# A transformer block on one core: memory pieces in a bank of their own, one filling rate, and another order at the start

## The chip, the cores and the metric

The kernel runs on one core of a Trainium2 chip. The metric is the device time of one execution in microseconds (us), less is better. The engines are named as the profile names them: PE (TensorE, matmuls), PEld (its weight loads), DVE (VectorE), ACT (ScalarE), POOL (GpSimd) and SP (SyncE, which here only issues DMAs). Each engine works through its own queue in order; semaphores tie the queues together. SBUF is the on-chip memory, PSUM the eight banks into which PE writes its results.

## The reference

One block with adaptive layer norm, an attention with a compressive memory, and a gated linear unit. x has 2048 rows of 512; there are 32 heads of 16; the rows form 4 segments of 512. All is fp32.

```python
mod = (silu(c) @ w_mod).reshape(1, 6, 1, 512)      # sa, ca, ga, sb, cb, gb
h = layernorm(x) * (1 + ca) + sa
q, k, v = heads(h @ wq), heads(h @ wk), heads(h @ wv)
for s in range(4):                                  # segments, in order
    logits = qs @ ks.T * 16 ** -0.5 + causal_mask
    a_dot  = softmax(logits) @ vs
    a_mem  = (phi(qs) @ M) / (phi(qs) @ z + 1e-6)   # phi(t) = t + 1 if t > 0 else exp(t)
    out[s] = g * a_mem + (1 - g) * a_dot            # g = sigmoid(beta)
    M, z   = M + phi(ks).T @ vs, z + sum(phi(ks))
x = x + ga * (out @ wo)
h = layernorm(x) * (1 + cb) + sb
x = x + gb * (((h @ w_gate) * (h @ w_up)) @ w_down) # 1376 inner columns
```

## The kernel before

**Accuracy.** Matmuls of the projections and of the GLU part run in a reduced fp32 format, each operand split into a high and a low half (names ending in H and L), so each product is three matmuls: high x high, low x high, high x low. Query and key go to DRAM as three bf16 parts each and come back stacked along the contraction.

**Stages.** At the start (L400 to L702) the kernel loads x of segment 0, the first two modulations (wm0), and the projection weights, in the order v, k, q. `mod0` (L464) makes shift and scale, `ln` (L107) the normalized and transposed h of segment 0, `load_w` (L481) the halves of the weights (ACT rounds the high half, POOL, for two pieces of v DVE, subtracts). Then PE computes V of segment 0 (`a_v`, L498) and key and query of head group 0 (`a_kq`, L518). A head group is 8 heads, 128 columns; there are 4 in a segment, and `a_kq(s, g, nm)` also makes phi of key or query for the memory.

Then comes the attention loop (L708). A *unit* is 4 heads of one segment; there are 32 units, and the loop variable v is the unit whose keys are worked on. Each turn has five *slots*. In a slot stand, in PE's order: query logits for the maxima of a later unit (`q_step`, L190: matmuls q<-kst,qst and, at the end of the slot, the mask matmuls q<-cmask), key logits of unit v (`k_step`, L244; ACT takes the exponential L262, POOL cuts the triangle L265), the products with V (`av_step`, L269, tile tb), and then the filling. `q_step` writes one PSUM tile of two banks (tag lq, one buffer), and DVE's reduction L226 (tile mxb) empties it; the next slot's q waits for that. In slot 2 `n_step` (L230) transposes the maxima into the bank sm (tile ntp), in slot 4 `t_step` (L293) transposes the output there (tile tr).

**The filling.** What else PE must do is written as generators that yield an estimated cost in us: `fill_a` (L630) for the segments' norms, projections and memory, `fill_b` (L649) for the weights of wo, the output projection (`wo_seg`, tiles op and wops) and the second norm. After each slot `fill` (L672) adds rate/5 to a credit and takes pieces until it is used up. The rate is 10.0 before unit 0, 6.6 up to turn 22, and 4.8 from there. `until` forces what a coming unit needs. The order of all these matmuls on PE is fixed by a chain of dependencies (`pe`, L46); a scheduler orders the other engines' instructions.

**Memory pieces.** `a_mem(s, g)` (L560) has up to four: mp transposes phi(k) and ACT copies it (pkr); up 0 and up 1 multiply phi(q) with the memory MZ, and DVE's four operations L580 to L583 empty each into mem; mz multiplies pkr with V, and DVE (and POOL) add it to MZ. In `fill_a` all of `a_mem(s, g - 1)` follows the key projection of group g, that of the last group follows the next segment's norm. Each piece asks `bank` (L71) for a PSUM bank, as the projections do; in the loop that is the tag ms, two buffers in turn. V of the next segment comes before its first key projection, and waits (`vfree`) until the loop has left the buffers of V.

**The rest.** After the loop come the output projection of segment 3 and the GLU part (L754 to L796) over 4 segments and 11 column chunks.

Of the kernel before, what the change touches and what calls it, by code (L numbers as in the profile page):

```python
# [8 lines left out]
F32 = mybir.dt.float32  # L9
# [8 lines left out]
P = 128  # L18
S, D, H, DH, NSEG, L, F = 2048, 512, 32, 16, 4, 512, 1376
KT = D // P  # L20
NG = 4
HG = 8
# [9 lines left out]
def tile_kernel(ctx, tc, x, wq, wk_, wv, wo, beta, w_gate, w_up, w_down, c, w_mod, out):  # L32
# [74 lines left out]
    def ln(pool, hpool, xt, s, sc, sh, pfx, hb, fast):  # L107

        mv = pool.tile([P, 4, 2], F32, tag="mv", name=f"{pfx}mv{s}", bufs=2)
        for t in range(4):  # L110
            st = pool.tile([P, 6], F32, tag="st", name=f"{pfx}st{s}_{t}", bufs=2)
            nc.vector.bn_stats(st, xt[t])
            nc.vector.bn_aggr(mv[:, t, :], st)  # L113
        sd = pool.tile([P, 4], F32, tag="sd", name=f"{pfx}sd{s}", bufs=2)
        nc.scalar.activation(sd, mv[:, :, 1], AF.Sqrt, bias=epst[:, 0:1])
        y = pool.tile([P, 4], F32, tag="y", name=f"{pfx}y{s}", bufs=2)
        nc.vector.reciprocal(y, sd)
        a = pool.tile([P, 4], F32, tag="ya", name=f"{pfx}ya{s}", bufs=2)
        b = pool.tile([P, 4], F32, tag="yb", name=f"{pfx}yb{s}", bufs=2)
        eng = nc.gpsimd  # L120
        eng.tensor_mul(a, y, y)
        eng.tensor_scalar(b, mv[:, :, 1], 1.0, EPS, op0=ALU.mult, op1=ALU.add)  # L122
        eng.tensor_mul(b, b, a)
        eng.tensor_scalar(b, b, -0.5, 1.5, op0=ALU.mult, op1=ALU.add)
        eng.tensor_mul(y, y, b)
        yield 0.4
        for t in range(4):
            nc.vector.tensor_scalar(xt[t], xt[t], mv[:, t, 0:1], y[:, t:t + 1],
                                    op0=ALU.subtract, op1=ALU.mult)
        yield 0.4  # L130
        hH, hL = [], []
        for d in range(KT):
            ps = bank(f"{pfx}tp{s}_{d}")
            for t in range(4):
                TP(ps[:, t * P:(t + 1) * P], xt[t][:, d * P:(d + 1) * P], ident)
            h = pool.tile([P, L], F32, tag="hf", name=f"{pfx}hf{s}_{d}", bufs=hb[2])
            nc.scalar.activation(h, ps, AF.Identity, scale=sc[:, d:d + 1], bias=sh[:, d:d + 1])
            hi = hpool.tile([P, L], F32R, tag=hb[0].format(d), name=f"{pfx}hH{s}_{d}", bufs=hb[1])
            lo = hpool.tile([P, L], F32R, tag=hb[0].format(4 + d), name=f"{pfx}hL{s}_{d}", bufs=hb[1])
            if fast:  # L140
                nc.vector.tensor_copy(hi, h)
                nc.vector.tensor_sub(lo, h, hi.bitcast(F32))
            else:
                nc.scalar.activation(hi, h, AF.Copy)
                nc.gpsimd.tensor_sub(lo, h, hi.bitcast(F32))
            hH.append(hi)
            hL.append(lo)
            yield 0.45
        return hH, hL
# [40 lines left out]
    def q_step(u, i):  # L190
# [5 lines left out]
        def mm(c, h, qb, k0, n, b=None, stop=False):  # L196
            b = h % 2 if b is None else b
            MM(qp[:, b, c:c + n * P], Q[0:96, h, qb * P:(qb + 1) * P], K[0:96, h, k0 * P:(k0 + n) * P],
               start=True, stop=stop, skip_group_check=True)

        src = qp.rearrange("p b (j t) -> p (b j) t", t=P)
        if i == 4:
# [260 lines left out]

    def mod0():  # L464
        for j in range(2):
            a0 = mod_acc(r0[j])
            ps = bank(f"m0_{j}", shape=(P, 4))
            for i in range(4):
                MM(ps[:, i:i + 1], a0[:, i * P:(i + 1) * P], ones[:, 0:1], start=True, stop=True)
            nc.vector.tensor_copy(sa_c[:, 2 * j:2 * j + 2], ps[:, 0:2])  # L470
            nc.vector.tensor_scalar_add(ca_c[:, 2 * j:2 * j + 2], ps[:, 2:4], 1.0)

# [8 lines left out]
    def load_w(nm, w, nst):  # L481
        wH[nm] = [pa.tile([P, D], F32R, name=f"w{nm}H{k}", bufs=1) for k in range(KT)]
        wL[nm] = [pa.tile([P, D], F32R, name=f"w{nm}L{k}", bufs=1) for k in range(KT)]
        wr = w.rearrange("(k p) n -> p k n", p=P)
        for k in range(KT):
            tg, n = stage[(nst + k) % len(stage)]
            raw = pa.tile([P, D], F32, tag=tg, name=f"wr{nm}{k}", bufs=n)
            nc.sync.dma_start(raw, wr[:, k, :])
            hi, lo = wH[nm][k], wL[nm][k]
            if nm != "v":  # L490
                hi, lo, raw = (hi.rearrange("p (g d h) -> p g h d", g=NG, h=HG),
                               lo.rearrange("p (g d h) -> p g h d", g=NG, h=HG),
                               raw.rearrange("p (g h d) -> p g h d", g=NG, h=HG))
            nc.scalar.activation(hi, raw, AF.Copy)
            eng = nc.vector if nm == "v" and k % 2 == 1 else nc.gpsimd
            eng.tensor_sub(lo, raw, hi.bitcast(F32))

    def a_v(s):  # L498
        hH, hL = hcur[0]
# [18 lines left out]
    def a_kq(s, g, nm):  # L518
# [4 lines left out]
        if True:  # L523
# [14 lines left out]
            nc.scalar.activation(q3[:, 0, :], f, AF.Copy)  # L538
            (nc.vector if fast else nc.gpsimd).tensor_sub(r, f, q3[:, 0, :])
            (nc.vector.tensor_copy if fast else nc.scalar.copy)(q3[:, 1, :], r)  # L540
            nc.gpsimd.tensor_sub(q3[:, 2, :], r, q3[:, 1, :])
            for r0, n, k in ((0, 3, 0), (3, 2, 0), (5, 1, 0)) if nm == "k" else ((0, 1, 3), (3, 1, 2), (5, 1, 1)):
                if nm == "k":
                    nc.sync.dma_start(dst[s][g][r0:r0 + n].rearrange("r p t -> p r t"), q3[:, 0:n, :])
# [15 lines left out]
    def a_mem(s, g):  # L560

        ph = phs.pop((s, g))
        if s < NSEG - 1:
            mp = bank(f"mp{s}_{g}")
            for t in range(4):
                TP(mp[:, t * P:(t + 1) * P], ph["k"][:, t * P:(t + 1) * P], ident)
            pkr = pa.tile([P, 4, P], F32, tag="pkr", name=f"pkr{s}_{g}", bufs=1)
# [2 lines left out]
        if s > 0:  # L570
# [1 line left out]
            mem = pa.tile([P, 4, HG, DH], F32, tag="mem", name=f"mem{s}_{g}", bufs=1)  # L572
            gb = gg[:, g * HG:(g + 1) * HG]
            for i in range(2):
                up = bank(f"up{s}_{g}_{i}", shape=(P, 2, HG, VS))
                for t in (2 * i, 2 * i + 1):
                    MM(up[:, t % 2].rearrange("p h e -> p (h e)"), ph["q"][:, t * P:(t + 1) * P],
                       MZ[g].rearrange("p h e -> p (h e)"), start=True, stop=True)
# [6 lines left out]
                yield 0.5  # L585
            nc.sync.dma_start(memd[s][g], mem.rearrange("p t h e -> p (t h e)"))
        if s < NSEG - 1:
            mz = bank(f"mz{s}_{g}", shape=(P, HG, VS))
            for t in range(4):
                MM(mz.rearrange("p h e -> p (h e)"), pkr[:, t, :],  # L590
                   vt[s % 2][t][:, g * HG * VS:(g + 1) * HG * VS], start=t == 0, stop=t == 3)
# [24 lines left out]
    def open_b():  # L616
# [5 lines left out]
        for k in range(KT):  # L622
# [4 lines left out]
            nc.gpsimd.tensor_sub(woL[:, k, :], raw, woH[:, k, :].bitcast(F32))  # L627
            yield 0.3

    def fill_a():  # L630
        for s in range(NSEG):
            if s > 0:
                yield from a_ln(s)
                yield from a_mem(s - 1, NG - 1)
                while vfree[0] < s:
                    yield None
                yield from a_v(s)
                if s < 3:
                    yield from a_mod(s - 1)
            for g in range(1 if s == 0 else 0, NG):  # L640
                yield from a_kq(s, g, "k")
                if g > 0:
                    yield from a_mem(s, g - 1)
                if g == 2 and s + 1 < NSEG:
                    xts[s + 1] = xload(s + 1)
                yield from a_kq(s, g, "q")
        yield from a_mem(NSEG - 1, NG - 1)

    def fill_b():  # L649
        yield from open_b()  # L650
# [42 lines left out]
    next(lng)  # L693
    next(lng)
    mod0g()
    hcur[0] = run(lng)
    load_w("v", wv, 0)
    load_w("k", wk_, 4)
    load_w("q", wq, 8)
    run(a_v(0))  # L700
    run(a_kq(0, 0, "k"))
    run(a_kq(0, 0, "q"))  # L702
    btag[:] = ["ms"]
    load(0)
    load(1)
    until(0, 1)
    SL = 5.0
    for v in range(-2, NQ + 1):  # L708
        rate[0] = 10.0 if v < 0 else 6.6 if v < 23 else 4.8
        if 2 <= v + 3 < NQ:  # L710
            until((v + 3) // 8, (v + 3) // 2 % 4)
            load(v + 3)
# [112 lines left out]
```

## Time and profile before

| | us |
|---|---|
| three runs | 1060.09, 1062.77, 1066.46 |
| median | 1062.77 |
| profiled execution, whole | 1065.12 |
| its span, first to last instruction | 1063.4 |
| first query logits begin | 65.73 after the span's start |
| stretch from 692 to 1064, the GLU part | 372 |

The profile comes from one execution. The page gives the busy time of each engine and the share of the clock that PE was granted, in 40 slices; the list of waits gives, for two instructions, how long one engine sat idle until the other released it, how often, and the longest; a window's row gives for a stretch of the span the busy time and the number of instructions of each engine in turn, and at its end the granted clock, the share of the DMA engines and the GB/s. In a timeline a row is: start, length, engine, line, operation, out<-in, and in brackets the idle time before it with what ended it. The span is 1.7 us shorter than the execution's own time.

### The profile page before, as it was taken

How to read it: one execution, taken by the hardware profiler on the slowest of the kernel's cores; microseconds unless marked ns; L12 is line 12 of the kernel's file. 1: busy time of each engine (PE TensorE's matmuls, PEld its weight loads, DVE VectorE, ACT ScalarE, POOL GpSimd, SP SyncE). 2: the span in 40 equal slices, each digit the busy share in tenths (PEclk: the TensorE clock that was granted, in tenths of full speed). 3: DMA queues.
4: the chain of work that ended last, by engine and by line, in shares of the span. 5: the costliest groups of instructions: out<-in, count | busy, mean ns of one | idle time of the engine just before them, and what ended most of it. 6: DMA issues, size and time to landing. Idle time of an engine off the chain costs nothing.

```text
span 1063.4 us, 14282 instructions
## 1 busy us (share of the span) xinstructions
PE 946.1 (89%) x5496; PEld 656.4 (62%) x5496; DVE 495.8 (47%) x842; ACT 401.4 (38%) x564; POOL 301.2 (28%) x440
## 2 busy tenths in 40 slices
PE   5877998877988879998787989899999999999997
PEld 3555555554555544655444555688878878878885
DVE  8435564556554553555557554266523322322112
ACT  4335365553565553555435364223211211121111
POOL 6335143342153341354633242145400000000000
PEclk7789898989999987999799999999999999999999
DMA  7185334443244332255755422263220101011011
GB/s 235 48 254 165 93 116 124 144 154 102 79 154 144 100 105 66 77 167 182 238 174 154 122 71 74 73 180 90 83 80 1 40 15 65 3 38 40 1 40 39
DMA packets 83140, 109.81 MB, mean 103 GB/s; under 512 B 9504, under 2 KB 54560, under 8 KB 83072
## 3 DMA queue, kind: packets, MB, share of 16 engines
q1 hardware_dynamic: 82928, 108.89, 32.9%
q8 instruction: 43, 0.70, 0.3%
q14 instruction: 25, 0.20, 0.1%
q10 hardware_dynamic: 144, 0.02, 0.0%
HBM read 67.98 MB, written 40.63 MB: 102 GB/s over the span
## 4 chain that ended last, share of the span: by engine, by line
PE 73%; DVE 13%; DMA 5%; ACT 4%; issue 2%; POOL 2%; SPq 0%; DVEq 0%; ACTq 0%; POOLq 0%
PE gps L769 11%; PE ups L769 11%; PE q L54 10%; DVE mxb L226 7%; PE tb L54 6%; PE k L54 6%; PE vps L54 4%; PE qps L54 3%; PE kps L54 3%; PE wops L54 3%; PE acc3lq L782 1%; PE acc1lk L782 1%; PE acc1lq L782 1%; PE acc0lq L782 1%; PE acc2lk L782 1%
## 5 line engine op out<-in xcount | busy, mean ns | idle before, releaser
L226 DVE TENSOR_REDUCE mxb<-q 128x8 f32<-128x1024 f32 x160 | 195.6, 1223 | 215.3 <-PE q L54 215.2
L262 ACT ACTIVATE pt<-k 128x1024 f32<-128x1024 f32 x160 | 163.7, 1023 | 253.6 <-PE k L54 229.9
L265 POOL TENSOR_SCALAR_AFFINE_SELECT pt<-pt 128x256 f32<-128x256 f32 (+1 forms) x224 | 101.2, 466 | 282.2 <-ACT pt L262 280.2
L54 PE MATMUL q<-kst,qst 96*128 96x128 bf16 (+2 forms) x640 | 103.9, 287 | 52.4 <-DVE mxb L226 47.0
L774 DVE TENSOR_TENSOR gs<-gs,ups 128x512 f32<-128x512 f32 (+1 forms) x44 | 30.2, 687 | 187.9 <-PE ups L769 187.1
L54 PEld LDWEIGHTS <-qst 96*128 96x128 bf16 x640 | 52.6, 101 | 94.8 <-issue 86.4
L54 PE MATMUL k<-qst,kst 98*128 98x384 bf16 (+3 forms) x512 | 102.9, 315 | 2.2 <-ACT pt L262 2.1
L54 PE MATMUL tb<-pt,v 128*32 128x512 f32 (+3 forms) x1024 | 92.4, 457 | 0.5 <-POOL pt L265 0.5
L777 ACT ACTIVATE mH<-gs 128x512 fp32r<-128x512 f32 (+1 forms) x44 | 27.8, 631 | 160.8 <-DVE gs L774 160.8
L769 PE MATMUL ups<-chH,uH 128*128 128x512 f32 (+1 forms) x176 | 69.3, 394 | 0.0
L769 PE MATMUL gps<-chH,gH 128*128 128x512 f32 (+1 forms) x176 | 69.3, 395 | 0.0
L769 PE MATMUL ups<-chL,uH 128*128 128x512 f32 (+1 forms) x176 | 69.1, 393 | 0.0
L769 PE MATMUL gps<-chH,gL 128*128 128x512 f32 (+1 forms) x176 | 69.1, 392 | 0.0
L769 PE MATMUL gps<-chL,gH 128*128 128x512 f32 (+1 forms) x176 | 69.0, 392 | 0.0
L769 PE MATMUL ups<-chH,uL 128*128 128x512 f32 (+1 forms) x176 | 69.0, 392 | 0.0
L773 ACT ACTIVATE gs<-gps 128x512 f32<-128x512 f32 (+1 forms) x44 | 26.2, 599 | 107.0 <-PE gps L769 106.9
L54 PEld LDWEIGHTS <-kst 98*128 98x128 bf16 x512 | 48.0, 102 | 29.8 <-issue 9.6
L54 PEld LDWEIGHTS <-identb 128*128 128x128 bf16 x320 | 23.8, 101 | 64.9 <-issue 61.1
L54 PE MATMUL q<-cmask,identb 128*128 128x128 bf16 (+1 forms) x320 | 57.5, 263 | 0.0
L54 PEld LDWEIGHTS tb<-pt,v 128*32 128x32 f32 x1024 | 22.8, 111 | 37.3 <-issue 33.1
L778 DVE TENSOR_TENSOR mL<-gs,mH 128x512 fp32r<-128x512 f32 (+1 forms) x44 | 31.8, 723 | 28.2 <-ACT mH L777 28.1
L122 POOL TENSOR_SCALAR cyb<-cmv 128x4 f32<-128x4 f32 x4 | 0.8, 195 | 137.7 <-DVE cmv L113 137.6
(243 smaller groups left out, 1850.0 us busy)
## 6 DMA issues: line engine op xcount, KB each, us to landing
kst<-kd SPq DMA_DIRECT2D x32, 384.0 KB, 4.7
qst<-qd SPq DMA_DIRECT2D x32, 384.0 KB, 5.2
wm<-in_w_mod_dram SPq DMA_DIRECT2D x24, 256.0 KB, 3.2
kd<-k SPq DMA_DIRECT2D x16, 384.0 KB, 2.7
qd<-q SPq DMA_DIRECT2D x16, 384.0 KB, 2.7
x<-in_x_dram SPq DMA_DIRECT2D x16, 256.0 KB, 4.4
kd<-k SPq DMA_DIRECT2D x16, 256.0 KB, 2.1
qd<-q SPq DMA_DIRECT2D x16, 256.0 KB, 3.0
```

Source lines behind the costliest of these rows:

```text
L54: return pe(nc.tensor.matmul(*a, **k))
L122: eng.tensor_scalar(b, mv[:, :, 1], 1.0, EPS, op0=ALU.mult, op1=ALU.add)
L226: nc.vector.tensor_reduce(o, src, axis=AX.X, op=ALU.max)
L262: nc.scalar.activation(pt, kp, AF.Exp, scale=0.25)
L265: sels[u, i] = nc.gpsimd.affine_select(w, w, pattern=[[0, w.shape[1]], [1, P]], compare_op=ALU.is_ge, fill=0.0, base=0, channel_multiplier=-1)
L769: nc.tensor.matmul(ps[0:n], a[:, k, 0:n], b[k], start=j == 0, stop=j == 11)
L773: nc.scalar.activation(gs[0:n], pss[0][0:n], AF.Copy)
L774: nc.vector.tensor_mul(gs[0:n], gs[0:n], pss[1][0:n])
L777: nc.scalar.activation(mH[0:n], gs[0:n], AF.Copy)
L778: nc.vector.tensor_sub(mL[0:n], gs[0:n], mH[0:n].bitcast(F32))
L782: nc.tensor.matmul(acc[t], a[0:n, t * P:(t + 1) * P], b[0:n, :], start=i == 0 and j == 0, stop=i == NF - 1 and j == 2)
```

## The change

In words:

- `a_mem`: its tiles mp, up and mz are put into the tag sm (one buffer, that of ntp and tr) and no longer ask `bank`.
- `fill_a`: a new generator `inter(a, b)` takes a step of a, then a step of b, in turn. The memory pieces of the group before are taken in turn with the steps of a key projection, those of a segment's last group with the steps of the next segment's norm. V of segments 1 to 3 and the modulations move behind key and query of group 0.
- The filling rate is 5.7 in all turns from unit 0 on.
- Start: the weights are loaded in the order k, q, v; the k weights are asked for before the norm's transposes; key and query of group 0 come before V; group 1 is no longer forced ahead of the loop. All low halves of the weights are subtracted on DVE, and the last bf16 part of group 0's key and query too; five small operations of the first norm move from POOL to DVE.
- `mod0`: the weighted sum over the four blocks of wm0 is no longer made by DVE (eight operations) and followed by matmuls with a column of ones; each block is multiplied with its column of s_c on PE, four matmuls that accumulate.
- `q_step`: only the first matmul of a bank carries the start flag.

```diff
-        eng = nc.gpsimd
+        eng = nc.vector if pfx == "a" and s == 0 else nc.gpsimd
...
-               start=True, stop=stop, skip_group_check=True)
+               start=c == 0, stop=stop, skip_group_check=True)
...
     def mod0():
         for j in range(2):
-            a0 = mod_acc(r0[j])
             ps = bank(f"m0_{j}", shape=(P, 4))
             for i in range(4):
-                MM(ps[:, i:i + 1], a0[:, i * P:(i + 1) * P], ones[:, 0:1], start=True, stop=True)
+                for k in range(KT):
+                    MM(ps[:, i:i + 1], r0[j][k][:, i * P:(i + 1) * P], s_c[:, k:k + 1],
+                       start=k == 0, stop=k == KT - 1)
...
-            eng = nc.vector if nm == "v" and k % 2 == 1 else nc.gpsimd
-            eng.tensor_sub(lo, raw, hi.bitcast(F32))
+            nc.vector.tensor_sub(lo, raw, hi.bitcast(F32))
...
-            nc.gpsimd.tensor_sub(q3[:, 2, :], r, q3[:, 1, :])
+            (nc.vector if fast else nc.gpsimd).tensor_sub(q3[:, 2, :], r, q3[:, 1, :])
...
-            mp = bank(f"mp{s}_{g}")
+            mp = pst((P, 512), "sm", f"mp{s}_{g}")
...
-                up = bank(f"up{s}_{g}_{i}", shape=(P, 2, HG, VS))
+                up = pst((P, 2, HG, VS), "sm", f"up{s}_{g}_{i}")
...
-            mz = bank(f"mz{s}_{g}", shape=(P, HG, VS))
+            mz = pst((P, HG, VS), "sm", f"mz{s}_{g}")
...
+    def inter(a, b):
+        for w in a:
+            yield w
+            w = next(b, None)
+            if w is not None:
+                yield w
+        yield from b
+
     def fill_a():
+        mem = iter(())
         for s in range(NSEG):
             if s > 0:
-                yield from a_ln(s)
-                yield from a_mem(s - 1, NG - 1)
-                while vfree[0] < s:
-                    yield None
-                yield from a_v(s)
-                if s < 3:
-                    yield from a_mod(s - 1)
+                yield from inter(a_ln(s), mem)
+                mem = iter(())
             for g in range(1 if s == 0 else 0, NG):
-                yield from a_kq(s, g, "k")
-                if g > 0:
-                    yield from a_mem(s, g - 1)
+                if s == 0 and g == 1:
+                    mem = a_mem(0, 0)
+                yield from inter(a_kq(s, g, "k"), mem)
                 if g == 2 and s + 1 < NSEG:
                     xts[s + 1] = xload(s + 1)
                 yield from a_kq(s, g, "q")
-        yield from a_mem(NSEG - 1, NG - 1)
+                if s > 0 and g == 0:
+                    while vfree[0] < s:
+                        yield None
+                    yield from a_v(s)
+                    if s < 3:
+                        yield from a_mod(s - 1)
+                mem = a_mem(s, g)
+        yield from mem
...
     mod0g()
+    load_w("k", wk_, 0)
     hcur[0] = run(lng)
-    load_w("v", wv, 0)
-    load_w("k", wk_, 4)
-    load_w("q", wq, 8)
-    run(a_v(0))
+    load_w("q", wq, 4)
     run(a_kq(0, 0, "k"))
     run(a_kq(0, 0, "q"))
+    load_w("v", wv, 8)
+    run(a_v(0))
...
-    until(0, 1)
...
-        rate[0] = 10.0 if v < 0 else 6.6 if v < 23 else 4.8
+        rate[0] = 10.0 if v < 0 else 5.7
```

## The prediction, as it was put on record

> **What bounds the kernel now.** I read the page first, then what TensorE (PE) waits for, then the execution cut into stretches.
>
> ```profile
> PE 946.1 (89%) x5496; PEld 656.4 (62%) x5496; DVE 495.8 (47%) x842; ACT 401.4 (38%) x564; POOL 301.2 (28%) x440
> PEclk7789898989999987999799999999999999999999
> ```
>
> No engine is near full but PE, and PE's granted clock is below full only in the first two thirds. So there are two programs in one: a GLU part that PE fills, and an attention part with holes. The waits of PE say what the holes are:
>
> ```profile
> PE q L54 <- DVE mxb L226: 47.0, 58, 2.8
> PE mz L54 <- DVE mem L583: 18.5, 7, 3.0
> ...
> PE q L54 <- DMA qst<-qd: 4.6, 1, 4.6
> ...
> PE up L54 <- DVE phq L554: 3.1, 1, 3.1
> ```
>
> The first line is the cycle of the attention loop: one slot computes query logits (q) into a single PSUM tile, VectorE (DVE) reduces it (L226), and the next slot's q may start only then; what PE does meanwhile is the filling. The second line is the memory pieces. The other two are single waits that come up below. Stretches (columns: length, busy time with instructions for PE, PEld, DVE, ACT, POOL, then the clock); but for the first and the last, each is one unit of five slots, from the end of one unit's last reduction to the next's:
>
> ```profile
> 89.60:646.90 557.30, 476.51 (x3354) 289.04 (x3353) 310.00 (x535) 279.89 (x376) 209.99 (x323) 0.94 0.42 128
> 162.10:184.40 22.30, 18.94 (x119) 11.67 (x119) 10.96 (x23) 9.34 (x14) 7.12 (x12) 0.85 0.39 128
> 184.40:205.30 20.90, 17.30 (x122) 10.85 (x121) 10.83 (x22) 10.58 (x16) 7.11 (x11) 0.92 0.42 127
> 205.30:225.80 20.50, 17.41 (x121) 10.90 (x120) 11.17 (x23) 9.42 (x15) 7.32 (x12) 0.92 0.40 119
> 225.80:248.70 22.90, 15.57 (x119) 9.69 (x119) 16.24 (x32) 13.53 (x20) 12.56 (x15) 0.93 0.67 207
> 318.70:339.90 21.20, 18.06 (x124) 11.49 (x123) 11.40 (x24) 11.21 (x17) 8.55 (x13) 0.92 0.38 125
> 355.40:377.50 22.10, 16.81 (x121) 10.39 (x119) 11.03 (x24) 11.94 (x18) 8.59 (x13) 0.92 0.36 120
> 377.50:396.90 19.40, 13.60 (x103) 7.44 (x104) 10.84 (x21) 8.29 (x11) 8.09 (x13) 0.90 0.27 82
> 396.90:419.40 22.50, 19.85 (x103) 10.76 (x103) 7.65 (x12) 6.32 (x7) 2.94 (x8) 0.63 0.13 36
> 339.90:355.40 15.50, 15.37 (x116) 9.70 (x115) 8.09 (x13) 10.18 (x16) 7.71 (x11) 1.00 0.44 137
> 419.40:435.30 15.90, 15.90 (x115) 9.77 (x114) 7.67 (x12) 6.76 (x9) 4.24 (x9) 1.00 0.30 82
> 435.30:451.30 16.00, 15.87 (x113) 9.53 (x112) 7.75 (x13) 9.81 (x14) 6.30 (x10) 1.00 0.37 115
> 299.70:318.70 19.00, 15.89 (x123) 10.19 (x122) 10.40 (x24) 11.37 (x17) 9.51 (x14) 1.00 0.56 176
> 451.30:470.70 19.40, 17.47 (x117) 11.04 (x117) 9.93 (x21) 9.83 (x15) 8.97 (x12) 0.91 0.55 163
> 486.70:507.20 20.50, 17.10 (x116) 10.72 (x115) 12.06 (x26) 10.97 (x16) 10.49 (x14) 0.88 0.59 184
> 692.00:1064.00 372.00, 365.13 (x1608) 294.95 (x1606) 122.30 (x195) 69.33 (x111) 41.98 (x42) 1.00 0.17 51
> ```
>
> A unit that carries projections alone takes 15.5, 15.9 or 16.0 us with the clock at 1.00: I take 15.8 as the floor. The six units with memory pieces (rows two to seven) take 20.5 to 22.9, and the two that follow, where the filling waits for its turn, 19.4 and 22.5. The loop's 30 units take 557.3; at the floor they would take 30 x 15.8 = 474. So 83 us of excess is there to be had or kept. The last row, the GLU part, is untouched: 372 us stay.
>
> What makes a memory unit long, on PE and then on DVE:
>
> ```profile
> 161.07 1.09 PE L54 MATMUL up<-MZ,phq 128*128 128x136 f32 x8
> 165.14 2.15 PE L54 MATMUL mz<-v,pkr 128*128 128x136 f32 x8 [2.97 <-DVE mem L583]
> 167.08 1.06 PE L54 MATMUL q<-kst,qst 96*128 96x256 bf16 x4
> ```
> ```profile
> 160.83 1.22 DVE L226 TENSOR_REDUCE mxb<-q 128x8 f32<-128x1024 f32 x1 [1.23 <-PE q L54]
> 161.97 0.24 DVE L309 RECIPROCAL rd<-tr 128x16 f32<-128x16 f32 x1
> ...
> 164.57 0.76 DVE L583 TENSOR_TENSOR mem<-up,den 128x256 f32<-128x256 f32 x2
> ```
>
> Both up pieces and mz are issued in one slot, on two banks that rotate. mz waits until DVE has emptied an up bank, behind the reduction and the tr work: 2.97 us idle, with q of the next slot queued behind it on PE. Afterwards the clock is down: eight mz steps take 2.15 us where eight up steps took 1.09.
>
> **The change part by part.** (1) *Memory pieces.* They move to bank sm, one piece between two chunks of a key projection, so one per slot. The work is the same; the wait changes. sm has one buffer, shared with ntp (slot 2) and tr (slot 4). No row shows that, so I bound a piece's wait: below by 0, where a whole slot (15.8 / 5 = 3.2 us) lies between two users of sm; above by 161.97 to 165.33 = 3.4 us, what DVE took to empty tr and two ups. In the built instruction order most pieces have their slot alone. Where one follows ntp (six times) or tr (three times), it waits for the reduction of 1.22 and two or three short operations, about 1.9 or 2.7 us, of which a projection chunk of three covers 0.7 and the reduction would have been waited for anyway: 1.0 and 1.9 us more. One slot holds ntp, up and mz: 3.6. The piece waits at the head of PE's queue, and behind it stand the rest of the filling and the next q; DVE's reduction waits for that q. With 0.3 for each of the 27 others and 4 for the last group, whose up still follows its own query projection (3.1 in the waits), the 40 pieces of segments 1 to 3 cost 6 + 5.7 + 3.6 + 8 + 4 = 27 us. Now the six memory units cost 22.3 + 20.9 + 20.5 + 22.9 + 21.2 + 22.1 - 6 x 15.8 = 35; with the three smaller ones (299.70, 451.30, 486.70: 3.2 + 3.6 + 4.7 = 11.5) it is 46. Gain 46 - 27 = 19 (between 0 and 40).
>
> (2) *One filling rate, V after the first key and query projections.* 6.6 and 4.8 per unit become 5.7. The order before has 17 slots of the loop without filling, the order after has 5. Units 377.50 and 396.90 exceed the floor by 3.6 + 6.7 = 10; I give back 9. The two rates are near each other, so the hiding itself stays: 5.7 / 5 = 1.1 per slot is five projection matmuls, and at 2.73 / 12 = 0.23 us (row below) they fit under the reduction of 1.22. The holes while wo and od are fetched stay: their order is the same. Two segments' modulation loads keep their place ahead of a reduction on DVE's queue, and SP's queue still holds the reload of kst and qst behind them: unchanged. With 2 us for smaller shifts the part gives 11 (3 to 14); the 27 us of excess that are in neither part stay.
>
> In the stretch 396.90 to 419.40 the granted clock is 0.63, and the idles of PE in it are no longer than this one:
>
> ```profile
> 401.86 1.01 PE L54 MATMUL q<-kst,qst 96*128 96x128 bf16 x8 [1.31 <-DVE mxb L226]
> ```
>
> The Trainium skill, "TensorE: Matmul & The Clock Gate", Part 1, says half rate comes after an idle window of about 3.4 us. By the page this stretch would owe its length to idle time alone, and part (2) would give about 5 us less; the trace decides here.
>
> (3) *The start.* Rows of the chain, then ScalarE's (ACT):
>
> ```profile
> 35.57 11.60 PE vps L54 x38
> 47.17 2.73 PE kps L54 x12
> 57.31 4.00 DMA qd<-q
> 61.38 4.31 DMA qst<-qd
> 65.73 1.26 PE q L54 x4
> ```
> ```profile
> 14.05 2.66 ACT L494 ACTIVATE wvH<-wrv 128x512 fp32r<-128x512 f32 x4 [4.05 <-DMA wrv<-in_wv_dram]
> 16.76 3.03 ACT L494 ACTIVATE wkH<-wrk 128x512 fp32r<-128x512 f32 x3
> 23.10 0.78 ACT L137 ACTIVATE ahf<-atp,modc 128x512 f32<-128x512 f32 x1 [3.31 <-PE atp L57]
> ```
>
> V goes out of the path to the first q: key and query come straight after the norm. The norm itself hardly comes earlier: on ACT's queue the first ahf now stands behind eight strided weight pieces of 3.03 / 3 = 1.01 and one plain one of 0.66, 14.05 + 8.7 = 22.8 against 23.10, and four ahf and one weight piece later it is 26.4. DVE is relieved of eight modulation sums and takes ten subtractions of weights that POOL did; I estimate the last low half at 30 to 31 and the key projection's end at 31.5, against 47.17 + 2.73 = 49.9. From there to the first q is 65.73 - 49.9 = 15.8 now. I add 4.5, since the low part of k waits on DVE behind the second norm's square root on ACT, and its four normalizations: qst lands at about 52. The 24 more small modulation matmuls lie ahead of the transposes, but these must wait for the norm and the weights anyhow: nothing, or 3 us if that cover is gone.
>
> But then PE is late: V's second and third weight pieces now come behind the loads of x and of kd on SP, and behind q's low part on DVE, at about 42.5. From there 42 matmuls at 0.23 to 0.31 (11.60 / 38), one key projection (2.73) and two memory steps (1.4) make 56 to 60. I take 58: 7.7 us earlier than 65.73, and 2 more since PE no longer comes cold from 4.6 idle us. Fifteen projection matmuls that stood ahead of q go into the loop: 15 x 0.23 = 3.4 back. Net 6 (between 0 and 14).
>
> (4) The accumulate flag of q (start only at c = 0) and five norm operations on DVE instead of POOL change no count on the path: 0.
>
> The sum: 19 + 11 + 6 = 36. The profiled execution took 1065.1 us, its span 1063.4, the median is 1062.8, so 2.3 less. 1062.8 - 36 = 1026.8; I say **1026**.
>
> **The rivals.** *Slower: the one bank.* sm becomes the bound: pieces queue behind ntp and tr, each emptied by DVE only behind a reduction, and PE stops shortly in most slots. It decides from 36 / 40 = 0.9 us per piece (40 pieces in segments 1 to 3) beyond what I have counted. At half of the 3.4 us in the rows above, 1.7 in place of 0.7, it costs 40; with the clock at 0.92 of the memory units kept in 16 units (16 x 15.8 x 0.08 = 20) it gives 1026 + 60 = 1086. For it: PE already loses 47 us to DVE's reductions. Against: DVE is 47% busy, and the order leaves most pieces a slot. The Trainium skill, "TensorE: Matmul & The Clock Gate", section on psum-queue depth-cycling, says that short idles at each bank change make the clock swing; if that holds here, this rival does. 0.12.
>
> *No gain: the waits move.* The pieces cost in slots 2 and 4 what they cost together, and the start is held by V's late weights (0 of part 3): within 1057 to 1068. 0.08.
>
> *Part of it:* the start gives nothing and a piece costs 1.2: 1026 + 6 + 20 = 1052; 1040 to 1057. 0.16.
>
> *More:* pieces cost nothing beyond the floor, the first q starts when qst lands (52): 1026 - 21 - 6 = 999; below 1010. 0.10.
>
> *It does not do what it says:* the even rate would leave slots empty as before. The built order speaks against it (5 for 17); it is in "no gain".
>
> **How the numbers follow.** My forecast, 1010 to 1040, has 0.54. A run of this kernel can tell about 0.5% (5.3 us). Faster: 0.54 + 0.10 + 0.16 = 0.80; same 0.08; slower 0.12. The range leaves out the slower rival and half of the larger gain: 1004 to 1056.
>
> **What would show it.** Units with memory pieces at 16.5 to 18.5 us in place of 20.5 to 22.9, and the wait of mz for mem gone from PE's list, with short waits of up or ntp for DVE in its place; the clock at 1.00 through units 15 and 16; first q near 58, not 66. I am wrong if PE waits over 2 us at sm in most units, or if the first q stays after 64.

## The result and the profile after

| | before | after |
|---|---|---|
| median of the runs, us | 1062.95 | **1052.24** |
| range of the four runs, us | 1060.09 to 1066.46 | 1050.08 to 1053.56 |
| profiled execution, whole | 1065.12 | 1052.66 |
| its span | 1063.4 | 1050.9 |

The ratio is 0.9896, with a 95% interval of 0.9861 to 0.993: 10.7 us less, where 36 were forecast. The page of the profile after first, busy time and clock:

```profile
PE 950.7 (90%) x5544; PEld 658.7 (63%) x5544; DVE 491.3 (47%) x851; ACT 406.8 (39%) x566; POOL 278.7 (27%) x423
...
PEclk7899999989989999999789999999999999999998
```

The clock still dips: near 230 and 300 us, where memory pieces stand, and from 500 to 550 us, where the last up and the first op stand. What PE waits for, after (columns: us in total, times, the longest):

```profile
PE q L54 <- DVE mxb L226: 43.8, 65, 3.1
PE up L54 <- DVE phq L554: 6.5, 3, 3.2
PE up L54 <- DVE nt L240: 6.0, 5, 1.5
PE up L54 <- DVE orow L312: 4.8, 3, 2.0
PE ntp L57 <- DVE mem L583: 4.0, 1, 4.0
...
PE mp L57 <- DVE nt L240: 3.1, 2, 1.7
...
PE mz L54 <- DVE nt L240: 2.0, 1, 2.0
```

Of the 18.5 us of mz behind mem, 0.5 is left. In their place up, mp and mz wait for nt (L240, the emptying of ntp) and for orow (L312, the emptying of tr): 6.0 + 4.8 + 3.1 + 2.0 = 15.9 us, all for the one buffer of sm. One ntp waits there too, for 4.0 us, until DVE has emptied an up. And phi of the query (L554) is now waited for three times instead of once: in segment 3 no mp comes first, so the first up of a group stands only one step (three matmuls) behind the end of its own query projection.

Stretches of after, cut as in the prediction; the first is the loop's 30 units, then one unit each (4, 7, 8, 12, 14, 15, and for comparison 17):

```profile
81.60:631.90 550.30, 469.98 (x3339) 281.44 (x3339) 308.88 (x536) 283.22 (x377) 209.80 (x325) 0.95 0.43 130
151.40:171.80 20.40, 17.23 (x118) 10.44 (x118) 13.43 (x32) 11.61 (x15) 6.88 (x16) 0.92 0.28 94
204.30:221.50 17.20, 15.44 (x117) 9.87 (x118) 10.51 (x22) 8.37 (x12) 6.20 (x11) 1.00 0.46 127
221.50:242.90 21.40, 17.22 (x122) 11.34 (x121) 10.51 (x22) 13.15 (x19) 9.50 (x14) 0.84 0.28 86
294.50:318.60 24.10, 17.66 (x121) 10.76 (x120) 13.61 (x32) 12.33 (x16) 7.10 (x16) 0.86 0.26 78
336.20:355.70 19.50, 17.60 (x120) 11.04 (x121) 10.22 (x20) 11.43 (x17) 8.72 (x13) 0.91 0.42 130
355.70:375.50 19.80, 16.89 (x116) 9.81 (x116) 10.22 (x23) 8.27 (x11) 7.04 (x12) 0.91 0.44 127
392.90:408.60 15.70, 14.98 (x109) 8.79 (x108) 7.84 (x13) 9.88 (x16) 9.22 (x13) 1.00 0.45 135
```

The span's 12.5 us are 8.0 ahead of the loop (81.60 for 89.60, where the forecast had 7.7 for the first q and 2 more), 7.0 in its 30 units (550.3 for 557.3, where parts (1) and (2) were forecast to take 30 out and the start to put 3.4 back), and 2.5 given back behind it. Units of 16.5 to 18.5 were forecast for the memory pieces. Segments 1 and 2 have ten units with such pieces: of the six shown (unit 17 has none), five are at 19.5 to 24.1, and the other four, units 5, 6, 13 and 16, took 16.6, 15.9, 17.6 and 17.4. The start, PE's rows: V's weights come late, and the first q begins at 57.57:

```profile
37.23 0.79 PE L54 MATMUL vps<-wvH,ahH 128*128 128x512 f32 x1 [2.97 <-ACT wvH L495]
...
41.51 0.79 PE L54 MATMUL vps<-wvL,ahH 128*128 128x512 f32 x1 [1.77 <-DVE wvL L496]
...
57.57 0.61 PE L54 MATMUL q<-kst,qst 96*128 96x512 bf16 x2
...
58.41 0.39 PE L54 MATMUL qps<-ahH,wqL 128*128 128x512 f32 x1
```

One of the long units from near, unit 4. PE, then DVE:

```profile
162.68 1.10 PE L54 MATMUL up<-MZ,phq 128*128 128x136 f32 x4 [1.51 <-DVE nt L240]
163.41 0.79 PE L54 MATMUL kps<-ahH,wkH 128*128 128x512 f32 x1
164.00 0.63 PE L54 MATMUL kps<-ahH,wkL 128*128 128x512 f32 x1
```
```profile
160.90 1.22 DVE L226 TENSOR_REDUCE mxb<-q 128x8 f32<-128x1024 f32 x1 [0.15 <-PE q L54]
162.04 0.27 DVE L239 CAST nt<-ntp 16x128 bf16<-16x128 f32 x1
162.35 0.28 DVE L240 TENSOR_TENSOR nt<-ntp,nt 16x128 bf16<-16x128 f32 x1
```

up stands behind ntp in sm, DVE empties ntp only after the reduction, and PE is idle for 1.51 us. That part was foreseen. What follows was not priced: the projection matmuls behind the wait take 0.63 to 0.79, where one at full clock takes 0.39 (the row at 58.41). The wait is paid once, and then the matmuls run at half the clock: the granted clock is 0.50 from 162.90 to 166.31, for 3.41 us.

### The profile page after: what moved, and what is told of

Same layout as the page of the kernel before. It is cut to its first block, busy times and chain, and to the rows that moved or that the text cites. A ratio compares the mean times of both kernels' runs of the same rounds, so it can differ in the third digit from the quotient of the medians.

```text
span 1050.9 us, 14370 instructions
## 1 busy us (share of the span) xinstructions
PE 950.7 (90%) x5544; PEld 658.7 (63%) x5544; DVE 491.3 (47%) x851; ACT 406.8 (39%) x566; POOL 278.7 (27%) x423
## 4 chain that ended last, share of the span: by engine, by line
PE 73%; DVE 12%; DMA 7%; ACT 4%; issue 2%; POOL 1%; SPq 1%; DVEq 0%; ACTq 0%; POOLq 0%
PE gps L780 12%; PE ups L780 12%; PE q L54 10%; DVE mxb L226 8%; PE tb L54 6%; PE k L54 6%; PE vps L54 3%; PE wops L54 3%; PE qps L54 2%; PE kps L54 2%; DMA wm<-in_w_mod_dram 2%; PE acc3lk L793 2%; PE acc3lq L793 2%; PE acc1lq L793 1%; PE acc1lk L793 1%
## 5 line engine op out<-in xcount | busy, mean ns | idle before, releaser
L54 PE MATMUL q<-kst,qst 96*128 96x128 bf16 (+2 forms) x640 | 101.3, 283 | 44.3 <-DVE mxb L226 43.8
L54 PE MATMUL k<-qst,kst 98*128 98x384 bf16 (+3 forms) x512 | 100.1, 309 | 1.8 <-ACT pt L262 1.7
L789 DVE TENSOR_TENSOR mL<-gs,mH 128x512 fp32r<-128x512 f32 (+1 forms) x44 | 31.8, 723 | 28.2 <-ACT mH L788 28.1
L780 PEld LDWEIGHTS ups<-chL,uH 128*128 128x128 f32 (+1 forms) x176 | 32.6, 186 | 7.9
```

The lines of the kernel that those rows point to most:

```text
L54: return pe(nc.tensor.matmul(*a, **k))
L780: nc.tensor.matmul(ps[0:n], a[:, k, 0:n], b[k], start=j == 0, stop=j == 11)
L789: nc.vector.tensor_sub(mL[0:n], gs[0:n], mH[0:n].bitcast(F32))
```

## The experiments

Theory A: the price of sm (its one buffer, and the half clock behind each wait) eats what the rest gains. Theory B: part (1) gained, and the even rate lost it, since it crowds the last third of the loop. The kernel before ran in each set; its medians were 1062.8 to 1064.9, and I use 1064. Two of my own measures recur. A *unit's excess* is the time between the ends of two units' last reductions less 15.8; and "ms" means that the three tiles ask `bank` again.

**The start alone** (kernel before with the new order of the weights, `mod0`, and key and query first):

```diff
-    load_w("v", wv, 0)
...
-    run(a_v(0))
+    load_w("q", wq, 4)
     run(a_kq(0, 0, "k"))
     run(a_kq(0, 0, "q"))
+    load_w("v", wv, 8)
+    run(a_v(0))
```

> The kernel before with the new start alone (weights in the order k, q, v, key and query of group 0 ahead of V, modulation by TensorE, low halves on DVE, group 1 not forced); filling order, rates and banks as before. In the changed kernel the unit -1 ends 8.0 us earlier than before. If the start is worth just this, 1063 - 8 = 1055. If the start is given back in the loop (15 projection matmuls more to fill), 1059 to 1063.

Measured: 1065.63, ratio 0.999 (0.9958 to 1.0021): nothing. In the profile the first q begins 7.5 us earlier, and most of this is lost in one place: the last slot before unit 0 takes 10.9 us, where it took 4.7. ACT, then PE, in this run:

```profile
76.34 0.60 ACT L534 ACTIVATE kf<-kps 128x512 f32<-128x512 f32 x1
81.01 0.63 ACT L538 ACTIVATE k<-kf 128x512 bf16<-128x512 f32 x1 [4.07 <-DMA kd<-k]
...
82.58 0.58 ACT L568 ACTIVATE pkr<-mp 128x512 f32<-128x512 f32 x1
```
```profile
83.22 1.50 PE L54 MATMUL mz<-v,pkr 128*128 128x136 f32 x5 [5.90 <-ACT pkr L568]
```

mz needs pkr, pkr stands on ACT's queue behind L538, and L538 waits 4.07 us for the DMA of an earlier key to leave its buffer. Unit 0 begins at 89.0 instead of 89.6.

**Pieces in ms, in turn** (after, with the bank alone undone):

```diff
-            mp = pst((P, 512), "sm", f"mp{s}_{g}")
+            mp = bank(f"mp{s}_{g}")
...
-                up = pst((P, 2, HG, VS), "sm", f"up{s}_{g}_{i}")
+                up = bank(f"up{s}_{g}_{i}", shape=(P, 2, HG, VS))
...
-            mz = pst((P, HG, VS), "sm", f"mz{s}_{g}")
+            mz = bank(f"mz{s}_{g}", shape=(P, HG, VS))
```

> The changed kernel with the memory pieces spaced as in it, but in the tag ms (the projections' two banks), so that ntp and tr keep sm for themselves. Theory A (the wait at the one buffer of sm behind ntp and tr, and the half clock after it, cost what the spacing gained): the waits of up, mp and ntp for DVE go, about 15 to 20 us less than the changed kernel's 1052, so 1032 to 1037. Theory B (the loss sits in the even rate, which crowds the last third): no change, 1050 to 1054.

Measured: 1024.04, ratio 0.9621 (0.9601 to 0.9641). The bank costs 28.2 us, more than A said.

**Pieces kept out of slots 2 and 4** (after; `inter` skips a piece there):

```diff
             yield w
+            if cslot[0] in (2, 4):
+                continue
             w = next(b, None)
```

> The changed kernel, with pieces taken in turn with a projection only in slots 0, 1 and 3, not in slot 2 (behind ntp) or 4 (behind tr). Theory A: most of the waits behind ntp and tr go, a few slots get two pieces; 10 to 14 us less, 1038 to 1042. Theory B: 1050 to 1054.

Measured: 1058.3, ratio 0.9952 (0.9924 to 0.9979): a miss, 6 us worse than after. Pieces that are put off come two and three to a later slot and then wait for each other: mz for mem 10.6 us in three waits. In the profiled execution (1054.0, the shortest of ten) the 30 units take 548.6 us, 1.6 less than in after, and unit 0 begins 3.1 later (84.7 for 81.6), behind a wait of mz for pkr of 4.8 us. Putting the pieces off in this way is no remedy.

**Part (1) alone undone** (after, with pieces in ms and together behind the key projection):

```diff
...
-                yield from inter(a_kq(s, g, "k"), mem)
+                yield from a_kq(s, g, "k")
+                if g > 0:
+                    yield from a_mem(s, g - 1)
...
```

> The changed kernel with part 1 alone undone: memory pieces in ms and all of a group's together behind the key projection, as before; start, V's place and the rate of 5.7 as changed. Theory A (part 1 is worth nothing, 46 us of excess before and after): 1049 to 1056. Theory B (part 1 gained about 15, the rate lost it): 1065 to 1070.

Measured: 1041.08, ratio 0.9782 (0.976 to 0.9804), below both theories. Part (1) as a whole costs 11.2 us (1052.2 - 1041.1): taking turns gains 17.0 (1041.1 - 1024.0), the bank loses 28.2.

**Part (2) alone** (kernel before, rate and order of V):

```diff
-        rate[0] = 10.0 if v < 0 else 6.6 if v < 23 else 4.8
+        rate[0] = 10.0 if v < 0 else 5.7
```

and the lines of `fill_a` that move V behind key and query of group 0.

> The kernel before with part (2) alone: the rate 5.7, and V of segments 1 to 3 and the modulations behind key and query of group 0; memory pieces together in the ms banks, the start, the weights' order and the flag as before. By the forecast's term of 11 us: 1052. If the start is worth nothing as long as the memory pieces of group 0 stand together ahead of the loop (a slot of 10.7 us there in the two runs that have the new start and the pieces together), all that the run with everything but part (1) gained, 23 us, comes from part (2): 1041 to 1044. If the start gave its 6 to 8 us in that run: 1047 to 1050.

Measured: 1044.34, ratio 0.98 (0.9754 to 0.9847): 20 us, where the forecast had 11. The start, with the flag of part (4), on top of it gives 3.3 (1044.3 - 1041.1), little more than the 2 us by which the kernel before differs from set to set.

**The old rates, with sm and with ms** (in after, and in the kernel of 1024.0):

```diff
-        rate[0] = 10.0 if v < 0 else 5.7
+        rate[0] = 10.0 if v < 0 else 6.6 if v < 23 else 4.8
```

> The changed kernel with the two old filling rates, 6.6 up to turn 22 and 4.8 after it, in place of 5.7. By the forecast's part (2), the even rate is worth about 9 us: 1061. By the rival, that the even rate only moves the holes (the last third of the loop grew by 9 and 6 us where the first two shrank, since op, wops and ctp now come two and three to a slot), it is worth nothing: 1049 to 1054. If the crowding it causes costs more than the holes it fills: below 1047.

> The changed kernel with its memory pieces in the ms banks, taken in turn with the key projections (the run that gave 1024.0), and with the old rates 6.6 and 4.8. If the even rate is worth what the forecast says, 9 us: 1033. If it only moves holes: 1022 to 1026. If it costs in the last third more than it gains: below 1021.

Measured: 1062.33, ratio 0.9981 (0.9941 to 1.0022), and 1036.07, ratio 0.9733 (0.9674 to 0.9791). The rate is worth 10.1 and 12.0 us in these two; it does not only move holes, and Theory B falls. The first of the two varies from 1055.5 to 1071.1, so its 10.1 is rough.

**Filling the waits at sm** (after, with six matmuls of zeros ahead of each piece that stands behind another user of sm in its slot; they are added work):

```diff
+        if cslot[0] in (2, 4) and smu[0]:
+            d = bank("d" + name)
+            for _ in range(6):
+                MM(d, dm[:, 0:P], dm, start=True, stop=True)
```

> The changed kernel with six matmuls of zeros (128x512 bf16, about 0.21 us each, 1.3 in all) ahead of each of the 11 memory pieces that stand in one slot behind another user of sm; they go to an ms bank and nobody reads them. They fill the time in which PE would wait for DVE to empty sm. Ten slots of the changed kernel that hold these pieces exceed their neighbours by 30 us, of which about 12 are idle and the rest is the granted clock of one half behind the idle. If the idle of 1.5 us is what takes the clock away: the clock stays, 1034 to 1042. If the clock goes down for another reason (the kind of work, a load over a longer window): 1050 to 1056, since the filled time was idle anyway; if the matmuls only add to the work, up to 1066.

Measured: 1046.13, ratio 0.9813 (0.9757 to 0.987): more work, and 6.1 us less. Four slots (unit 4, 8, 14 and 20; columns as above, PE's clock third from the end) in after:

```profile
162.13:169.28 7.15, 6.60 (x36) 4.23 (x36) 3.34 (x9) 3.68 (x6) 2.65 (x6) 0.76 0.28 93
230.95:240.45 9.50, 7.67 (x38) 5.39 (x39) 3.01 (x9) 3.15 (x4) 3.23 (x7) 0.64 0.08 28
336.23:343.28 7.05, 6.04 (x33) 4.11 (x34) 3.05 (x9) 3.44 (x6) 1.74 (x3) 0.76 0.54 163
440.58:447.90 7.32, 5.41 (x27) 2.56 (x28) 3.14 (x10) 1.02 (x1) 0.88 (x2) 0.77 0.33 102
```

with the filled waits:

```profile
161.15:166.50 5.35, 5.13 (x37) 3.25 (x36) 2.72 (x9) 3.31 (x6) 1.80 (x4) 1.00 0.23 74
228.66:235.95 7.29, 6.25 (x46) 3.94 (x45) 3.01 (x8) 3.15 (x4) 3.18 (x6) 1.00 0.11 37
333.45:339.00 5.55, 5.17 (x36) 3.20 (x35) 3.05 (x10) 3.08 (x5) 1.55 (x2) 1.00 0.66 207
434.73:440.44 5.71, 4.29 (x30) 2.24 (x28) 3.14 (x10) 1.02 (x1) 0.88 (x2) 1.00 0.40 128
```

and with the pieces in ms:

```profile
160.41:163.98 3.57, 3.57 (x29) 2.33 (x29) 2.49 (x9) 3.33 (x6) 1.83 (x4) 1.00 0.30 103
223.37:228.53 5.16, 3.73 (x30) 2.37 (x31) 2.78 (x8) 2.94 (x4) 3.19 (x7) 1.00 0.15 52
322.21:325.70 3.49, 3.49 (x28) 2.15 (x27) 2.60 (x10) 3.08 (x5) 1.56 (x2) 1.00 0.98 298
417.49:420.98 3.49, 2.75 (x22) 1.29 (x21) 2.73 (x9) 1.02 (x1) 0.88 (x2) 1.00 0.67 210
```

The matmuls of zeros bring the clock back to 1.00: the four slots take 23.9 instead of 31.0. Without the wait they take 15.7. So of the 15.3 us that sm costs here, 7.1 are half clock and 8.2 the wait itself; the idle time is what takes the clock away. These four are among the worst: all ten slots of the loop with a piece behind ntp or tr take 67.3 in after, 59.2 with the filled waits and 41.3 with the pieces in ms. Over the ten, half clock is 8.1 us of 26.0, and the wait itself is the larger part. Six of them ran below full clock in after; five of these came back to 1.00, and the sixth holds the ntp that waits 4.0 us, which nothing fills. The expectation's middle case, another cause, falls; its first size, 10 to 18 us, was too large.

**The start of before, with the pieces in ms and in turn** (the part of the change that the first experiment made alone, undone):

```diff
-    load_w("k", wk_, 0)
     hcur[0] = run(lng)
-    load_w("q", wq, 4)
+    load_w("v", wv, 0)
+    load_w("k", wk_, 4)
+    load_w("q", wq, 8)
+    run(a_v(0))
     run(a_kq(0, 0, "k"))
     run(a_kq(0, 0, "q"))
-    load_w("v", wv, 8)
-    run(a_v(0))
...
+    until(0, 1)
```

> The changed kernel with its memory pieces in the ms banks (1024.0) and with the start of the kernel before: weights in the order v, k, q, V first, group 1 forced ahead of the loop, the sums of the modulations on DVE, low halves on POOL. By the forecast's part (3) the new start is worth 6: 1030. If the 8 to 10 us by which the loop's first unit begins earlier in the profile are kept once the pieces of group 0 are taken in turn: 1032 to 1034. If a later wait takes them back, as in the run of the start alone: 1022 to 1026.

Measured: 1035.55, ratio 0.9744 (0.9687 to 0.98). Here the new start is worth 11.5 us, of which 7.5 lie ahead of unit 0 (87.4 and 79.9 at its begin).

**sm without taking turns** (the kernel of 1041.1 with the three tiles in sm; one of the three lines):

```diff
-            mz = bank(f"mz{s}_{g}", shape=(P, HG, VS))
+            mz = pst((P, HG, VS), "sm", f"mz{s}_{g}")
```

> The changed kernel with its pieces in sm, but all of a group's pieces together behind the key projection, as before: the bank without the turn-taking. With the pieces together in the ms banks it took 1041.1. If the single buffer of sm, emptied by DVE behind a reduction, is what costs: up 0, up 1 and mz of a group queue up behind each other, two waits of 1.5 to 2 us in each of the 10 groups more than with two buffers, and the clock with them: 1065 to 1090. If the cost in the changed kernel came from how turn-taking meets ntp and tr alone: 1041 to 1050.

Measured: 1089.36, ratio 1.0257 (1.0217 to 1.0297). Its waits of PE:

```profile
PE up L54 <- DVE mem L583: 12.7, 7, 3.1
PE mz L54 <- DVE mem L583: 10.4, 4, 5.2
PE mp L57 <- DVE nt L240: 7.7, 4, 2.7
```

The pieces queue behind each other for the one buffer, at 48 us.

**The last third** (the kernel of 1024.0, memory pieces of segment 3 beside the next query projection; then also op and ctp counted at 0.9):

```diff
-                yield from a_kq(s, g, "q")
+                yield from inter(a_kq(s, g, "q"), mem)
```

> The kernel that gave 1024.0, with two edits for the last third of the loop: the memory pieces of segment 3 are taken in turn with the query projection of the next group (one projection later), so that phi of the query has time to be made, and the pieces op and ctp are counted at 0.9 in place of 0.45, so that they come one to a slot. In the profile of that run four slots there wait for phi of the query (6.2 us in all) or for ACT (2.5), and the half clock behind them brings 21.1, 22.1, 23.1, 29.2 and 29.3 to about 15 us over their neighbours. If these holes are the cause: 10 to 12 us less in the loop, and 24 matmuls (5.5 us) that now come behind the loop: 1016 to 1020. If the waits only move to another piece: 1024 to 1030.

> The kernel that gave 1024.0, with only the first of the two edits of the run before: memory pieces of segment 3 in turn with the query projection of the next group, op and ctp counted as they were. In the run with both edits, units 20 to 22 took 47.0 in all, 6.9 less than the 53.9 of the kernel at 1024.0, and the rest of the loss lay in slots with op and ctp. If the two edits act apart: 1016 to 1019. If the gain of the first is given back at the loads of od, which are not moved (a wait of op for its DMA that grows by what the loop became shorter): 1022 to 1026.

Measured: both edits 1035.11 (ratio 0.9741, 0.9679 to 0.9802), the first alone **1022.12** (0.9587, 0.9522 to 0.9653), the shortest of all and below the kernels before and after. Units 20 to 22 take 52.2 in the kernel of 1024.0 and 47.4 in both of these (the 53.9 and 47.0 of the expectations were added up wrongly). Of the first edit's gain 1.9 us stay, little beside the two kernels' ranges (1020.26 to 1022.37 and 1022.82 to 1024.55), which come from two sets; units 0 to 3 and 24 to 29 exceed the floor by 3.0 and 2.1 more in its profile. Parting op and ctp was a mistake: units 24 to 29 grew by 10, with waits of 3 us in four of them.

**The rate alone, and the rate's effect without the rate** (kernel before, first the line with 5.7 only, then old rates and one number):

```diff
-                yield 0.5
+                yield 0.5 if i == 0 else 1.0
```

The second makes up 1 count for more, so that mz comes a slot later.

> The kernel before with the rate 5.7 in all turns and nothing else. By the forecast (9 of the 11 us of part (2) for the empty slots): 1054. If the rate's gain is that it parts mz from the two up pieces, most of the 18 us of part (2) come from it: 1044 to 1049.

> The kernel before with one number changed: the estimated cost of up 1 is 1.0 in place of 0.5, so that mz falls into the slot behind it in seven of the eight groups of segments 1 and 2; the rates stay 6.6 and 4.8, and 13 slots of the loop stay without filling (18 before). If three pieces in one slot are what makes the memory units long: six slots of 6.7 to 10.0 us become 4 to 5, 15 to 25 us less: 1038 to 1048. If the rate's gain lies in the filled slots: 1058 to 1064.

Measured: 1048.23 (ratio 0.984, 0.9782 to 0.9898) and 1054.99 (0.9903, 0.9871 to 0.9935). The rate alone gives 16 of the 20 us. For the second, three slots of the kernel before that stand behind up, up and mz (columns as above):

```profile
162.06:172.03 9.97, 6.69 (x28) 3.78 (x28) 4.79 (x14) 2.15 (x3) 2.63 (x4) 0.66 0.63 206
187.85:196.74 8.89, 5.62 (x39) 3.40 (x40) 4.41 (x11) 2.15 (x4) 2.85 (x4) 0.81 0.53 178
355.41:364.40 8.99, 5.51 (x28) 3.23 (x28) 4.79 (x14) 2.15 (x3) 2.64 (x4) 0.81 0.58 198
```

and the same with mz one slot later:

```profile
164.95:169.36 4.41, 3.40 (x25) 1.77 (x24) 4.41 (x14) 2.15 (x3) 2.16 (x3) 1.00 0.96 314
185.26:190.09 4.83, 3.87 (x40) 2.69 (x41) 3.83 (x11) 2.60 (x5) 2.26 (x3) 1.00 0.86 287
345.09:348.96 3.87, 3.50 (x29) 2.19 (x28) 3.35 (x10) 2.88 (x5) 2.42 (x4) 1.00 0.88 287
```

From 27.9 to 13.1 us, with the same banks and the same rates. In units 4 to 8, 12 to 16 and 20 to 23 together the excess falls from 61.8 to 37.6 (below). The kernel as a whole gained 9 us, less than I expected: unit 8 (8.2 of excess for 0.5; mz falls behind tr there and waits 3.6 us for DVE) and units 24 to 29 (below) give back 21. The units' excess, by parts of the loop:

| units | before | mz later | part (2) alone | after, pieces in ms, together | the same, in turn | after |
|---|---|---|---|---|---|---|
| 0 to 3 | 9.3 | 10.4 | 6.1 | 5.8 | 6.6 | 6.6 |
| 4 to 8 | 23.9 | 17.5 | 12.3 | 11.8 | 2.3 | 12.5 |
| 9 to 11 | 6.3 | 3.3 | 1.3 | 1.3 | 4.5 | 4.2 |
| 12 to 16 | 21.7 | 4.7 | 9.8 | 9.5 | 7.9 | 19.4 |
| 17 to 19 | 3.9 | 0.4 | 0.2 | 0.2 | 0.3 | 0.3 |
| 20 to 23 | 16.2 | 15.4 | 7.6 | 6.1 | 10.5 | 14.9 |
| 24 to 29 | 2.0 | 15.0 | 18.7 | 20.8 | 18.2 | 18.4 |
| all | 83.3 | 66.7 | 56.0 | 55.5 | 50.3 | 76.3 |
| unit 0 begins at | 89.6 | 91.3 | 92.1 | 89.1 | 79.9 | 81.6 |

## Why the prediction was wrong

**The direction was right, and the loss in size has one step: "Gain 46 − 27 = 19" in part (1).** Part (1) measured -11 (1041.1 to 1052.2), 30 us off, more than the whole miss of 26.

- *The 46.* I charged all that the memory units exceed the floor by to the pieces standing together, as if only part (1) could take it. But what made them long was three pieces in one *slot*, and that was set by the rate: at 6.6 a slot has 1.32, less what the piece before it overdrew, and up 0 and up 1 (0.5 each) mostly leave credit for mz; at 5.7 it has 1.14, and mostly they leave none. In the traces up 0, up 1 and mz share a slot in six of the eight groups of segments 1 and 2 before, and in one with 5.7. Part (2) alone takes the excess of units 4 to 8, 12 to 16 and 20 to 23 from 61.8 to 29.7. The one-number edit, which parts mz and leaves most of the empty slots as they were, takes it to 37.6; so most of it is the parting and not the filled slots. After part (2), taking turns had 17 us left to win, 9.2 of them ahead of unit 0 and 5.2 in the loop. Even with the old rates the 46 were not to be had: in the loop the excess is 83.0 with the new start alone and 63.3 with the old rates and the pieces in ms and in turn, which is 20 for taking turns together with the new place of V. With sm as well, the kernel at the old rates took 1062.3 for the 1065.6 of the new start alone: some 3 us, where 19 were forecast.
- *The 27.* The price of sm was nearly right as a sum: 23 without the last group's wait, 26.0 measured in the loop (76.3 - 50.3), 28.2 in the kernel's time. It was put together wrongly: ten slots with pieces behind ntp or tr carry the 26.0, where I had 15, and the 27 other pieces nothing, where I had 8. What I left out is the clock: in those ten slots it is 8.1 of the 26.0. But the 27 was set against an excess that was no longer there.

**Part (2), 11.** 20 measured, and 16 of them from the rate, for which I had written 9 for the empty slots. Of the two units whose empty slots I counted, 377.50 carries memory pieces as well (mp, both up and mz between 377.9 and 383.3), so it belonged to the 46 too. "The 27 us of excess that are in neither part stay" failed: units 24 to 29 went from 2.0 to 18.7, and the gains elsewhere hide this loss. There op and ctp now come two and three to a slot, but that this is the cause is not shown: the run that parted them lost 10 us more in these units.

**Part (3), 6.** The first q begins at 57.57, forecast 58, and V's weights do come late, as forecast (waits of 2.97 and 1.77). What the part is worth hangs on the others: nothing alone, 3 with part (2), 11.5 when the memory pieces of group 0 are taken in turn, because otherwise mz waits for ACT ahead of unit 0 (5.9 us in the first of these, 5.7 in the second). I had treated it as a term that adds.

**Part (4), 0,** was not tried by itself.

**The rivals.** "Slower: the one bank" came out in mechanism, in another kernel: 1089.4 with sm and without turns, for its 1086. That the two times are near is a coincidence: the rival's 60 stand on 1026, the 48 measured stand on 1041. In after the turns keep the pieces mostly apart, as I argued; where short idle times add up, they do take the clock down, as this rival says (last section). "Part of it" names 1052, the time that came out, but by luck and not for its reasons: it is 20 for part (2), 3 for the start and -11 for part (1), which is 12 of the kernel before's 1064.

**What would show it.** mz behind mem gone, short waits of up for DVE: right. Units at 16.5 to 18.5: right for about half of the ten, wrong for five at 19.5 to 24.1. Units 15 and 16: unit 16 ran at 1.00, unit 15 at 0.91, by a wait of mz at sm. The sign I named for the opposite, waits over 2 us at sm in most units, is not there either (one of 4.0): waits of 1.5 to 2 suffice.

## What to carry to other kernels

When two parts of a change could remove the same excess, don't give it to the one whose words describe it: ask what makes the excess, here which pieces fall into one slot, and price the second part on what the first leaves. A buffer that is emptied only behind a long operation of another engine is not made cheaper by spreading its users, if its other users already hold the slots; two buffers in rotation were worth 28 us here. And price a wait of PE with what follows it: here short waits that add up cost a further 3.4 us at half clock.

## What the runs showed of the hardware

A wait of PE inside the loop costs more than its length. I took every idle time of PE over 1 us between 90 and 630 us in six profiles (before, after, ms together, ms in turn, filled waits, and the kernel of 1022.1) that began at full clock, and read the granted clock in the 2.5 us behind it. Of 29 that lasted 2.4 us or more, 27 were followed by a clock below 0.95, most at 0.50 to 0.70. Of 32 between 1.5 and 2.4 us it was 16, and of 51 between 1.0 and 1.5 us it was 4; one of these is 1.21 us long, at 389.32 in the kernel before.

The length of a single wait does not decide, and the traces show what does. The clock changes only on a grid: in each of the sixteen profiles all its changes stand whole multiples of 3.41 us apart. Rows of the kernel before, cut at this grid (columns as above; the first number behind the length is PE's busy time):

```profile
386.10:389.52 3.42, 1.46 (x11) 0.90 (x11) 2.37 (x5) 1.02 (x1) 0.50 (x2) 1.00 0.01 2
389.52:392.93 3.41, 3.41 (x18) 1.03 (x17) 0.24 (x1) 1.02 (x1) 1.03 (x3) 0.50 0.02 2
392.93:396.34 3.41, 1.80 (x14) 1.21 (x14) 1.93 (x2) 0.82 (x1) 0.00 (x0) 1.00 0.00 0
396.34:399.76 3.42, 2.84 (x14) 0.91 (x13) 1.39 (x4) 1.09 (x2) 0.64 (x1) 0.50 0.68 217
...
409.99:413.41 3.42, 3.42 (x10) 2.31 (x9) 1.27 (x3) 0.45 (x1) 0.77 (x2) 0.50 0.02 2
413.41:416.82 3.41, 3.41 (x25) 1.93 (x24) 1.11 (x1) 1.39 (x2) 0.77 (x2) 1.00 0.00 0
```

The wait of 1.21 us shares its step with the end of another, and PE is idle for 3.42 - 1.46 = 1.96 us in all: the next step is at half clock. In that one PE is not idle, and the clock comes back. From 396.34 it stays at half for five steps, though no wait there is longer than 1.31 us: this is the stretch at 0.63 that the prediction showed. Only a step without idle time ends it. Counted over the same six profiles, by the idle time of PE summed over a step: of 740 steps at full clock with up to 1.5 us, one was followed by a step at half clock; of 26 with 1.5 to 1.8 us, 9; of 39 with more, all. Behind a step at half clock, the clock stayed there in all 27 cases with 0.5 us of idle or more, and in 5 of the 47 with less. The ends of matmuls are modelled in a profile, so these bounds are rough.

The Trainium skill, "TensorE: Matmul & The Clock Gate", Part 1, says that the clock halves after an idle window of about 3.4 us, and that the window runs freely. The trace agrees with the length and with the free running; it does not agree that the whole window must be idle. About half of it was enough here, in one wait or in several, and the measurement decides.
